# Two splits of hidden rows placed earlier in the order of the first down product

## The chip, the cores and the metric

The kernel runs on one core of a Trainium2 chip. The metric is the device time of one execution in microseconds, the median of several runs. A core has engines with a queue of instructions each, worked off in order: PE (TensorE, matrix products; its weight loads are shown as PEld), DVE (VectorE), ACT (ScalarE), POOL (GpSimd) and SP, which here issues DMAs.

## What is computed

An mLSTM cell over 4 batches, 8 heads, 768 positions and 40 features a head, and behind it a feed-forward block with exact GELU: 320 features up to 2048 and down again to 320, for all 3072 tokens.

```python
for t in range(S):
    m_new = np.maximum(f_gate[:, :, t] + m, i_gate[:, :, t])
    f_stab = np.exp(f_gate[:, :, t] + m - m_new)
    i_stab = np.exp(i_gate[:, :, t] - m_new)
    C = f_stab * C + i_stab * np.einsum('bhd,bhe->bhde', vt, kt)
    n = f_stab * n + i_stab * kt
    h_tilde = np.einsum('bhde,bhe->bhd', C, qt)
    y[:, :, t] = sigmoid(o_gate[:, :, t]) * h_tilde / np.maximum(np.abs(nq), 1.0)
x = y.transpose(0, 2, 1, 3).reshape(B * S, H * D)
h = x @ w_in
g = 0.5 * h * (1.0 + erf(h / sqrt(2)))
out = g @ w_out
```

## The kernel before, in words

The 768 positions are worked in 6 chunks of 128. In each chunk the four batches make 512 tokens. While the feed-forward block of one chunk runs on PE, the cell of a later chunk is worked beside it. The order in which every engine gets its work is written out by hand: strings of words (FRONT for everything up to the end of chunk 0's feed-forward, then SECOND, LATER, LAST) are read by `play` (line 1019), and each word calls one step. An engine's queue is the order in which the steps issue instructions for it. Waits are set where data or a buffer asks for them.

The steps around the change, all in the last lines of FRONT, by their letters:

- F: the next row of the first down product (line 880). There are 16 rows, of 128 hidden features each, from 0 to 15; the order below counts them. A row adds to the four banks `po`, one for each batch. Rows 0 to 9 take g and w_out as they are (4 products, two passes each). Rows 10 to 15 are taken in three parts (12 products): hi of g by hi of w_out, rest of g by hi of w_out, low of g by lo of w_out (lines 885 to 889).
- z n: split of g for row n (`split_g`, line 863): hi on ACT (line 873), rest on DVE (line 874), low on ACT (line 875). The parts go to tiles `g_part`, four parts in each, which lie where the g of earlier rows was: those of z10 where rows 0 to 3 were, later ones where rows 4 to 7 and 8 to 11 were.
- a n,k and b n,k: hi and lo of k rows of w_out from row n on (`out_hi`, line 931, on ACT for rows from 8 on; `out_lo`, line 938, on DVE).
- K and J: conversion of the next row of w_out from raw 64-bit words. K (`conv_one`, line 397) is two operations on ACT, `sig` (404) and `pow` (405), J (`conv_two`, line 410) two on DVE (416, 419). There are two buffers each for sig and pow, so the sig of one row waits until line 419 of the row two before it has read its buffer. The last J of FRONT are those of rows 12 to 15, the last K those of rows 14 and 15.
- X n, Y n, R n, G n: of chunk 1's cell, batch n: turn_y (transposes on PE into `px`, line 708, and x_hi on ACT, 718; two px banks), finish (DVE, lines 685 to 690, and 699), split_x (DVE, 727 and 728, which read px), gate (ACT, 506).
- p, + and [ and B: DMAs issued by SP; p exchanges halves of gate values, + copies k and q of later chunks, [ loads blocks, B loads the decay weights W, on which POOL then applies masks (line 474).

```python
        hi, rest, low = first_parts_of[n] = parts_of
        whole = first_g.row(n)
        nc.scalar.activation(out=hi, in_=whole, func=AF.Copy, scale=PART)
        nc.vector.tensor_tensor(out=rest, in0=whole, in1=hi, op=OP.subtract)
        nc.scalar.copy(out=low, in_=whole)
```

Of the kernel before, what the change touches and what calls it, by code (L numbers as in the profile page):

```python
# [27 lines left out]
    g1 c1 J y1 s2 K x0 t3 x1 v2 g2 O4 J B4 g3 c2 y2 s3 B5 K x2 K L5 J T0 K v3 A y3 M1 x3 c3 G0 M0 H O7 O6 O5 J  # L28
    J i5 u0 L6 u1 K W0 J W1 I4 A K S0 T1 C0 J i6 V0 i7 u2 G2 K U M2 L7 S1 J G1 K U i8 W2 J i9 C1 T2 K
    M3 f2 S2 V1 Y0 T3 J Y1 C2 e W3 K K K J S3 J C3 f3 K X0 J K R0 J K J V2 K Y2 J J K  # L30
    K V3 X1 J K r F J K (0 )0 F J K F K J F X2 G3 F J K F Y3 R1 J K F p + + + + J F J a10,2 b10,2 z10 a12 b12 F X3 z11 F a13,3 b13,3 z12 F z13 [1 F B8 z14 F B9 R2 z15 F R3 B10 B11 F a8 b8 a9 b9 F"""
CELL = "MWGVYXRKQDCSht"

HI_AT = {3: ("w_out3", 0), 8: ("w_out3", 2), 4: ("w_out0", 0), 5: ("w_out0", 1), 6: ("w_out2", 0), 7: ("w_out2", 1), 9: ("f0", 0)}
# [1073 lines left out]
```

## Time and profile before

| what | value |
|---|---|
| median of 3 runs | 438.06 us (437.81 to 439.68) |
| the profiled execution | 439.45 us |
| its span, first to last instruction | 437.7 us |
| PE, PEld busy | 429.5 us (98%), 376.6 us (86%) |
| DVE, ACT, POOL busy | 295.6, 277.3, 50.0 us |
| first down product on PE | 86.7 to 120.1 us |
| rows 10 to 15 of it | 108.75 to 120.1 us |
| mean granted clock of TensorE | 0.999 of full speed |

All times of the profile are microseconds from the start of the span of one profiled execution. A line of the order of time has the start, the duration, the engine, the line of the kernel, the operation, the tile written and the tiles read, the shape and the count; in brackets how long the engine was idle before it and what is taken to have released it. Neighbouring like instructions are merged into one line, and consecutive instructions of one engine overlap a little, so the step from one start to the next can be shorter than the duration. Who released a wait is inferred; "issue" means that nothing the profile shows was waited for.

### The profile page before, as it was taken

What the parts mean: (1) busy time and instruction counts of PE and PEld (TensorE: products, weight loads), DVE (VectorE), ACT (ScalarE), POOL (GpSimd) and SP (SyncE); (2) the same over time, 40 slices, a digit from 0 to 9 for tenths busy, and PEclk for the clock granted to TensorE, in tenths of its full rate; (3) what the DMA queues carried; (4) which work ended last, traced back from release to release, by engine and by line L of the source; (5) the groups of instructions that cost most, each with busy time, mean ns of one, the idle gap of its engine ahead of it and who ended that gap; (6) DMA issues with size and microseconds to landing.
All of it is one profiled execution on the core that took longest, in us unless ns stands there. A gap on an engine that the chain in (4) does not pass through costs nothing.

```text
span 437.7 us, 13034 instructions
## 1 busy us (share of the span) xinstructions
PE 429.5 (98%) x5344; PEld 376.6 (86%) x5344; DVE 295.6 (68%) x680; ACT 277.3 (63%) x595; POOL 50.0 (11%) x77
## 2 busy tenths in 40 slices
PE   9999999999999999999999999999999999999996
PEld 8778778877888898988898988898988889979986
DVE  7897777797888697737587737596746586533330
ACT  3989999965898985128776228795247715243441
POOL 3000212000530041030041030040010000000000
PEclk9999999999999999999999999999999999999999
DMA  7998996477791493563483564481561400010001
GB/s 153 198 211 228 196 247 164 124 197 197 210 184 56 88 191 63 108 172 63 65 179 69 107 165 69 94 157 32 108 157 18 61 1 1 18 45 1 1 1 60
DMA packets 162267, 48.81 MB, mean 112 GB/s; under 512 B 147776, under 2 KB 155232, under 8 KB 162208
## 3 DMA queue, kind: packets, MB, share of 16 engines
q1 hardware_dynamic: 161888, 47.65, 50.3%
q8 instruction: 42, 0.69, 0.7%
q10 hardware_dynamic: 320, 0.33, 0.2%
q14 instruction: 17, 0.14, 0.1%
HBM read 43.84 MB, written 9.37 MB: 122 GB/s over the span
## 4 chain that ended last, share of the span: by engine, by line
PE 73%; DVE 2%; ACT 2%; DMA 1%; issue 1%; ACTq 0%
PE po L991 31%; PE pu L966 24%; PE pu L977 7%; PE ps L568 3%; PE pf L621 2%; PE ph L674 1%; PE po L888 1%; PE po L674 1%; PE px L708 1%; DMA bits<-in_moe_w_out_dram 1%; PE pf L632 1%; ACT w_out_part L935 0%; DVE pow L416 0%; DVE w_out L419 0%; ACT sig L404 0%
## 5 line engine op out<-in xcount | busy, mean ns | idle before, releaser
L991 PE MATMUL po<-w_out_part,g_parts 128*128 128x320 f32 x960 | 140.7, 303 | 0.0
L991 PEld LDWEIGHTS po<-w_out_part,g_parts 128*128 128x128 f32 x960 | 131.6, 189 | 5.9 <-issue 4.6
L986 DVE TENSOR_TENSOR g_parts<-g_whole,g_parts 128x512 fp32r<-128x512 f32 x80 | 56.2, 702 | 57.8 <-ACT g_parts L985 55.7
L984 ACT ACTIVATE g_whole<-pu 128x512 f32<-128x512 f32 x80 | 47.2, 590 | 73.1 <-PE pu L977 62.6
L985 ACT ACTIVATE g_parts<-g_whole 128x512 fp32r<-128x512 f32 x80 | 50.5, 631 | 8.3 <-PE po L991 5.1
L474 POOL TENSOR_SCALAR_AFFINE_SELECT W<-W 128x1024 f32<-128x1024 f32 (+2 forms) x20 | 22.8, 1146 | 191.0 <-DMA W<-M_d 116.5
L500 ACT ACTIVATE W<-W,aT 128x128 f32<-128x128 f32 x128 | 38.7, 388 | 0.4 <-POOL W L474 0.2
L987 DVE CAST g_parts<-g_whole 128x512 fp32r<-128x512 f32 x80 | 36.3, 454 | 0.0
L699 ACT COPY far<-ob 128x128 f32<-128x128 f32 x16 | 4.6, 290 | 32.8 <-DVE ob L690 32.8
L966 PE MATMUL pu<-x_hi,w_in_hi 128*128 128x512 f32 x80 | 24.2, 384 | 0.0
L966 PE MATMUL pu<-x_hi,hi_first 128*128 128x512 f32 x80 | 23.9, 380 | 0.0
L966 PE MATMUL pu<-x_low,w_in 128*128 128x512 f32 x80 | 23.8, 379 | 0.0
L966 PE MATMUL pu<-x_rest,hi_first 128*128 128x512 f32 x80 | 23.8, 379 | 0.0
L966 PE MATMUL pu<-x_low,w_in_lo 128*128 128x512 f32 x80 | 23.8, 379 | 0.0
L966 PE MATMUL pu<-x_rest,w_in_hi 128*128 128x512 f32 x80 | 23.8, 379 | 0.0
L888 PE MATMUL po<-w_out,g 128*128 128x320 f32 x80 | 22.0, 432 | 0.0
L404 ACT ACTIVATE sig<-bits 128x320 f32<-128x320 f32 (+1 forms) x26 | 15.2, 585 | 10.6 <-issue 6.1
L574 DVE TENSOR_TENSOR W<-ps,W 128x256 f32<-128x256 f32 (+1 forms) x48 | 17.7, 413 | 4.2 <-PE ps L568 4.0
L888 PEld LDWEIGHTS po<-w_out,g 128*128 128x128 f32 x80 | 15.0, 190 | 5.9
L512 DVE STREAM_TRANSPOSE kT<-blocks 128x512 f32<-128x512 f32 x16 | 11.3, 709 | 12.0 <-DMA blocks<-kq_d 11.8
L639 DVE TENSOR_TENSOR far<-pf,gT 128x164 f32<-128x164 f32 x32 | 8.4, 319 | 14.7 <-PE pf L632 11.4
L1015 ACT ACTIVATE o_sb<-po 128x320 f32<-128x320 f32 x20 | 7.5, 442 | 16.7 <-PE po L991 16.7
(196 smaller groups left out, 788.3 us busy)
## 6 DMA issues: line engine op xcount, KB each, us to landing
W<-M_d SPq DMA_DIRECT2D x16, 512.0 KB, 6.6
bits<-in_moe_w_in_dram SPq DMA_DIRECT2D x20, 256.0 KB, 4.7
bits<-in_moe_w_out_dram SPq DMA_DIRECT2D x16, 320.0 KB, 4.8
blocks<-kq_d SPq DMA_DIRECT2D x32, 128.0 KB, 3.5
ob<-in_o_gate_dram SPq DMA_DIRECT2D x24, 160.0 KB, 4.3
out_dram<-o_sb SPq DMA_DIRECT2D x36, 80.0 KB, 2.0
wide<-M_d SPq DMA_DIRECT2D x4, 512.0 KB, 4.8
kq_d<-in_k_dram SPq DMA_DIRECT2D x6, 320.0 KB, 4.8
```

The costliest lines, as they stand in the source:

```text
L404: nc.scalar.activation(out=s, in_=hi.bitcast(F32), func=AF.Copy, scale=2.0 ** -112)
L474: nc.gpsimd.affine_select(out=x, in_=x, compare_op=OP.is_ge, fill=1.0e30, base=base, pattern=[[0, H], [1, x.shape[2]]], channel_multiplier=-1)
L500: nc.scalar.activation(out=W[n][:, h, :], in_=src, func=AF.Exp, scale=-1.0, bias=aT[:, self.c, r:r + 1])
L574: nc.vector.tensor_tensor(out=w[r, :, t], in0=ps[i][hip][r, :, t], in1=w[r, :, t], op=OP.mult)
L888: nc.tensor.matmul(to, xs[k][:, b * L:(b + 1) * L], w, start=(n == 0 and k == 0), stop=(n == NF - 1 and k + 1 == len(xs)), skip_group_chec ...
L966: nc.tensor.matmul(in_pairs(pus[i][e]), w3(at[k])[n][:, e, i * P:(i + 1) * P], in_turns(x3[n][:, k, :]), start=(n == 0 and k == 0), stop=F ...
L977: nc.tensor.matmul(in_pairs(pus[i][e]), w3(r)[n][h, p % 2, i * P:(i + 1) * P], in_turns(x3[n][h, NX, :]), start=False, stop=(n == 2), skip ...
L984: nc.scalar.activation(out=whole, in_=self.pus[n // 4][n % 4 // 2][n % 2], func=AF.Gelu)
L985: nc.scalar.activation(out=hi, in_=whole, func=AF.Copy, scale=PART)
L986: nc.vector.tensor_tensor(out=rest, in0=whole, in1=hi, op=OP.subtract)
L987: nc.vector.tensor_copy(out=low, in_=whole)
L991: nc.tensor.matmul(in_pairs(self.po[t]), x[:, t * L:(t + 1) * L], in_turns(w), start=(n == 0 and k == 0), stop=(n == NF - 1 and k == 2), s ...
```

## The change

In the last line of FRONT, two words change place. z10 moves from behind `a10,2 b10,2` to directly behind the fifth F (row 4). z12 moves from behind `a13,3 b13,3` to in front of them, behind the tenth F (row 9), and the F of row 10 stands behind a13 and b13 as before.

```diff
-    K V3 X1 J K r F J K (0 )0 F J K F K J F X2 G3 F J K F Y3 R1 J K F p + + + + J F J a10,2 b10,2 z10 a12 b12 F X3 z11 F a13,3 b13,3 z12 F z13 [1 F B8 z14 F B9 R2 z15 F R3 B10 B11 F a8 b8 a9 b9 F"""
+    K V3 X1 J K r F J K (0 )0 F J K F K J F X2 G3 F z10 J K F Y3 R1 J K F p + + + + J F J a10,2 b10,2 a12 b12 F X3 z11 F z12 a13,3 b13,3 F z13 [1 F B8 z14 F B9 R2 z15 F R3 B10 B11 F a8 b8 a9 b9 F"""
```

On the engines this means: on ACT the hi and low of z10 stand directly behind the gate of batch 3 (line 506) and in front of the sig of row 14; the hi and low of z12 stand in front of the hi of w_out rows 13 to 15. On DVE the rest of z10 stands in front of the conversion of row 12, and the rest of z12 in front of the lo of w_out rows 13 to 15. The orders on PE, POOL and SP stay as they are.

## The prediction, made before the changed kernel was run

> **What bounds the kernel now.** I read the busy table first, then the waits and the order of time between 94 and 126 us, where the moved steps lie, engine by engine.
>
> ```profile
> PE 429.5 (98%) x5344; PEld 376.6 (86%) x5344; DVE 295.6 (68%) x680; ACT 277.3 (63%) x595; POOL 50.0 (11%) x77
> ```
>
> PE is busy 98% of the span, and the chain that ended last is PE from 113.88 us on almost without a break. So the change is worth what it does to PE's gaps in the first down product, and what it makes late behind that. The weight loads of that stretch (start, duration, operation, count, idle before):
>
> ```profile
> 106.16 0.41 PEld L708 LDWEIGHTS px<-ident,ob 128*128 128x128 f32 x2
> 106.64 1.92 PEld L888 LDWEIGHTS po<-w_out,g 128*128 128x128 f32 x8
> 108.75 0.62 PEld L888 LDWEIGHTS po<-w_out_part,g_part 128*128 128x128 f32 x4 [0.19 <-ACT g_part L873]
> 109.96 3.29 PEld L888 LDWEIGHTS po<-w_out_part,g_part 128*128 128x128 f32 x24 [0.59 <-DVE g_part L874]
> 113.87 6.00 PEld L888 LDWEIGHTS po<-w_out_part,g_part 128*128 128x128 f32 x44 [0.63 <-DVE g_part L874]
> ```
>
> 106.64 is row 9; 108.75 the first four products (hi) of row 10; 109.96 the other 8 of row 10, row 11 and the hi of row 12; 113.87 the rest of row 12 up to row 15, ending at 119.87. Three gaps: 0.19 (hi of z10 on ACT), 0.59 (rest of z10 on DVE), 0.63 (rest of z12 on DVE, which stands behind b13): 1.41 us. These are what the two moved steps could remove.
>
> Where z10 goes, on DVE and on ACT:
>
> ```profile
> 98.89 0.50 DVE L419 SCALAR_TENSOR_TENSOR w_out<-sig,pow 128x320 uint32<-128x320 uint32 x1
> 101.12 0.49 DVE L416 SCALAR_TENSOR_TENSOR pow<-sig,pow 128x320 uint32<-128x320 uint32 x1 [1.74 <-ACT pow L405]
> 101.64 0.50 DVE L419 SCALAR_TENSOR_TENSOR w_out<-sig,pow 128x320 uint32<-128x320 uint32 x1
> 102.71 0.49 DVE L685 SCALAR_TENSOR_TENSOR ob<-ob,far 128x320 f32<-128x320 f32 x1 [0.57 <-ACT ob L506]
> 104.96 0.55 DVE L728 CAST x_low<-px 128x384 fp32r<-128x384 f32 x1
> 105.43 0.48 DVE L416 SCALAR_TENSOR_TENSOR pow<-sig,pow 128x320 uint32<-128x320 uint32 x1
> 105.94 0.50 DVE L419 SCALAR_TENSOR_TENSOR w_out<-sig,pow 128x320 uint32<-128x320 uint32 x1
> 108.48 0.83 DVE L943 TENSOR_TENSOR w_out_part<-w_out,w_out_part 128x640 fp32r<-128x640 f32 x1
> ```
> ```profile
> 102.22 0.46 ACT L506 ACTIVATE ob<-ob 128x320 f32<-128x320 f32 x1
> 102.57 0.49 ACT L404 ACTIVATE sig<-bits 128x320 f32<-128x320 f32 x1
> 106.53 0.50 ACT L404 ACTIVATE sig<-bits 128x320 f32<-128x320 f32 x1 [2.98 <-issue]
> 107.41 0.76 ACT L935 CAST w_out_part<-w_out 128x640 fp32r<-128x640 f32 x1
> 108.07 0.63 ACT L873 ACTIVATE g_part<-g 128x512 fp32r<-128x512 f32 x1
> ```
>
> From L685 at 102.71 to L419 at 105.94 DVE runs without a gap. ACT's sig at 106.53 (row 15) has a buffer that row 13's L419 read last; that ends at 105.94 + 0.50 = 106.44, so the 2.98 us put down to "issue" are a wait for DVE. Behind it in ACT's queue stands a10 (107.41), which row 10 needs as well as z10. So the stretch is a loop: DVE's queue sets row 15's conversion, that sets a10, and a10 sets row 10.
>
> **The change, part by part.** No instruction is added or removed, and no DMA moves. SP's, POOL's and PE's orders are the same; moved are three instructions of z10 and three of z12.
>
> z10, ACT: hi and low go ahead of row 14's sig, to where L506 leaves ACT at 102.57: hi 102.57 to 103.20, low 103.10 to 103.71 (steps of 0.53 and 0.51 between starts, as at 108.07). Their buffer needs rows 0 to 3, whose products ended at 95.3: no wait.
>
> z10, DVE: the rest now stands in front of row 12's L416 (101.12) and waits for the hi, 103.20 + 0.03 (as at 110.51 to 110.54) = 103.24. Behind it in DVE's queue are row 12's two operations, finish 3 (L685 to L699), split_x 1 (L727, L728), and rows 13 to 15. L416 goes from 101.12 to 103.84 (0.60 a step, from 109.22 to 109.82), L419 to 104.36, L685 to 104.78 (0.42 later, as from 95.83 to 96.25). L685 ran at 102.71, so the 0.57 it waited is absorbed and +2.07 remains. Nothing up to L419 of row 13 has a gap to take it up: L728 ends at 107.58, row 13's L419 at 108.51.
>
> What is late next: turn_y 3 (the px at 106.16) takes the bank that L728 reads, so it starts at 107.63 and not 106.16: PE loses 1.47. Row 9 then runs 108.11 to 110.03. Row 15's sig on ACT: 106.53 + 2.07 = 108.60, a10 109.48 to 110.24. Row 10 starts 0.05 behind it (the latency from 108.70 to 108.75): 110.29, a gap of 0.26. z10 is long done, but a10 is not.
>
> From there the steps run as before without z10: b10 on DVE 110.55 to 111.38; row 10's low needs it: 110.29 + 8 x 0.137 (3.29 us for 24 loads) = 111.39, so 0.04 lost. ACT: a12 110.14, X3 110.53, z11 hi 110.91, low 111.44. z11's rest on DVE 111.70 to 112.39, needed at 112.53.
>
> z12: on ACT hi 111.95, low 112.47, then a13 at 112.98 (before 110.91) to 114.10. On DVE its rest runs 112.62 to 113.31, ahead of b13, and row 12 needs it only at 114.2: the 0.63 is gone. The price: b13 starts at 114.13 (before 112.06) and z13's rest behind it (1.10 a step) at 115.24 to 115.93. Row 13 starts at 115.27 and needs that rest at 115.82: 0.16 lost. z14 (DVE from 115.84) and z15 (117.38 to 118.06) come before 117.1 and 118.7, when their rows start.
>
> Sum of PE's gaps: 1.47 + 0.26 + 0.04 + 0.16 = 1.93 instead of 1.41: **+0.52 us** at the end of the first down product.
>
> Behind it DVE ends that stretch some 1.2 us later (z15's rest 117.38 instead of 116.22). What hides that:
>
> ```profile
> 128.35 1.11 DVE L639 TENSOR_TENSOR far<-pf,gT 128x164 f32<-128x164 f32 x4 [1.24 <-PE pf L632]
> ```
>
> DVE waits 1.24 us here for PE, which comes 0.52 later itself: 1.2 - 0.52 is less than 1.24, cost nothing. Without that cover it would be 0.7. The masks on POOL follow DMAs that the moved work doesn't touch.
>
> Bounds. Lower: if DVE were held for nothing, all three gaps go, -1.41. Upper: the gaps return nothing and the whole +2.07 reaches the end. I take +0.52, since each of its four terms is set by a wait that the rows show.
>
> The one price the rows don't settle: b13, z13 and z14 now run beside POOL's masks (114.67, 4.08 us for three, 1.36 each). z14 and z15 ran there before, at 114.67 and 116.22, in 0.69 and 0.68 us; z10 and z11, away from the masks, took 0.69: nothing. The two L943 of 128x320 from 117.75 took 0.67 each instead of 0.49 at 109.82: 0.18 each. For three operations 0 to 0.5 us; I take 0, as the same operation beside the same masks shows. The Trainium skill (SBUF — State Buffer, Who interferes with whom) says that a DVE operation with two SBUF inputs and a GpSimd operation that reads SBUF shut each other out for a whole instruction. By that rule the sum would be +3.2 (below); the 0.69 beside the mask speaks against it here.
>
> The profiled execution took 439.45 us with a span of 437.70. The sum makes that 438.2 and 440.0. The median of the runs is 438.06, 1.39 below the profiled one; on it the forecast is 438.06 + 0.52 = **438.6 us**.
>
> **Rivals.**
> Free room: ACT sits idle 2.98 us, DVE 1.74 and 0.57, so z10 would fit in for nothing and the three gaps go: 438.06 - 1.41 = 436.65. For it: the idle times are real. Against: DVE's lie in front of a wait for ACT, and the hi can't come before 103.20.
>
> Passed on: DVE's +2.07 reaches the end, since later gaps move rather than go (a13 is 2.07 later on ACT, and rows 13 to 15 hang on it): 440.1. For it: z13's rest has no slack. Against: row 12's gap of 0.63 ends with z12 ahead of b13.
>
> Masks in the way: b13 and z13 each wait out one mask of 1.36 us on POOL, so row 13 and all behind it come 2.72 later than forecast: 441.3, slower by 0.7%. It decides from 114.67 on, when the masks begin. For it: the slower L943 at 117.75. Against: z14's 0.69 beside the first mask. (It is what the rule of the Trainium skill, SBUF — State Buffer, named above, would do here.)
>
> No effect: a10 comes early enough for row 10, if row 15's sig isn't held by row 13's L419; the 1.47 before row 9 and the 1.41 saved cancel: 438.1.
>
> **How the numbers follow.** Forecast 0.60 (438.1 to 439.3 for half a microsecond on either side), free room 0.08, passed on 0.17, masks 0.07, no effect 0.08. Half a per cent, 2.2 us, is about what a measurement of this kernel can tell from no change (its three runs span 437.81 to 439.68). Free room and no effect stay within it; I leave 0.03 for faster. Passed on is at the edge: half its chance, with the masks, makes 0.16 slower. Within: 0.81. The range reaches from near free room to just past passed on, 437.0 to 440.5, and leaves out the masks and part of free room.
>
> **What would show it.** z10's L873 near 102.6 and L874 near 103.2; row 12's L416 near 103.8; the px of turn_y 3 on PE after a gap of some 1.5 us, near 107.6; a10 (L935, 128x640) near 109.5 and row 10 directly behind its end; no gap ahead of row 12's rest; the first pu load near 120.3 instead of 119.82. Wrong if L685 stays near 102.7, if PE shows no gap ahead of turn_y 3, if L943 or L874 take over 1 us (128x512) beside the masks, or if PE shows new gaps behind 120 us.

## The result

The changed kernel took 439.82 us (median of 22 runs, 438.12 to 442.16), the kernel before 438.31 us (22 runs, 437.24 to 440.1). The ratio is 1.0027 with a 95% interval from 1.0016 to 1.0039: slower by 0.7 to 1.7 us. The forecast was 438.6 us, on a median of 438.06, that is 0.52 us slower or a ratio of 1.0012. The direction was right and the time lies in the range. The size is two to three times what was forecast (1.2 us by the ratio, 1.5 by the medians), and the time lies outside the half microsecond on either side of the forecast, 438.1 to 439.3, to which the prediction gave its chance of 0.60.

The span of the profiled execution is 438.9 us instead of 437.7. Row 0 of the first down product begins at 87.04 us, 0.33 later than before (86.71). That is ahead of the first moved step, so times are best read from row 0 on. The weight loads in order of time (start, duration, operation, count, idle before):

```profile
108.02 0.20 PEld L708 LDWEIGHTS px<-ident,ob 128*128 128x128 f32 x2 [1.62 <-issue]
...
110.61 8.53 PEld L888 LDWEIGHTS po<-w_out_part,g_part 128*128 128x128 f32 x61 [0.39 <-ACT w_out_part L935]
119.31 1.52 PEld L888 LDWEIGHTS po<-w_out_part,g_part 128*128 128x128 f32 x11 [0.17 <-DVE g_part L874]
120.78 0.33 PEld L966 LDWEIGHTS pu<-x_hi,hi_first 128*128 128x128 f32 x2
```

The gaps of 0.59 and 0.63 that the change was about are gone. In their place stand 1.62 ahead of turn_y 3, 0.39 ahead of row 10, now waiting for a10 (L935) and not for z10, and 0.17 within row 15, whose rest is late. The 61 loads behind row 10's gap hide 0.14 more, at row 13's rest: they take 8.53 us, where 0.1375 each (5.50 us for 40 in a profile below) makes 8.39. From row 0 to the first load of chunk 1's up product (here 120.78) it takes 33.74 us instead of 33.11.

DVE and ACT in order of time show the loop at work:

```profile
103.57 0.69 DVE L874 TENSOR_TENSOR g_part<-g,g_part 128x512 fp32r<-128x512 f32 x1 [3.12 <-ACT g_part L873]
...
105.11 0.48 DVE L685 SCALAR_TENSOR_TENSOR ob<-ob,far 128x320 f32<-128x320 f32 x1
...
107.36 0.55 DVE L728 CAST x_low<-px 128x384 fp32r<-128x384 f32 x1
...
108.34 0.50 DVE L419 SCALAR_TENSOR_TENSOR w_out<-sig,pow 128x320 uint32<-128x320 uint32 x1
```
```profile
108.92 0.50 ACT L404 ACTIVATE sig<-bits 128x320 f32<-128x320 f32 x1 [2.67 <-issue]
...
109.80 1.15 ACT L935 CAST w_out_part<-w_out 128x640 fp32r<-128x640 f32 x2
```

DVE stands idle for 3.12 us with z10's rest at the head of its queue, though row 12's words were ready on ACT by 100.44 (its L405 ran at 99.86 for 0.58). Row 13's L419 ends at 108.84, and row 15's sig starts 0.08 later: the wait called "issue" is that buffer. L728 ends at 107.91, and turn_y 3 starts 0.11 behind it.

What the forecast had at nothing is on POOL, and on DVE beside it:

```profile
116.10 1.09 POOL L474 TENSOR_SCALAR_AFFINE_SELECT W<-W 128x1024 f32<-128x1024 f32 x1 [48.99 <-ACT g_part L873]
```
```profile
116.13 1.60 DVE L874 TENSOR_TENSOR g_part<-g,g_part 128x512 fp32r<-128x512 f32 x1
```

z14's rest starts 0.03 us after a mask and takes 1.60 instead of 0.69 us. z15's rest comes late behind it, which is row 15's gap.

### The profile page after: what moved, and what is told of

Same layout as the page of the kernel before. It is cut to its first block, busy times and chain, and to the rows that moved or that the text cites. A ratio compares the mean times of both kernels' runs of the same rounds, so it can differ in the third digit from the quotient of the medians.

```text
span 438.9 us, 13035 instructions
## 1 busy us (share of the span) xinstructions
PE 429.6 (98%) x5344; PEld 375.8 (86%) x5344; DVE 297.4 (68%) x680; ACT 277.5 (63%) x595; POOL 50.9 (12%) x77
## 4 chain that ended last, share of the span: by engine, by line
PE 74%; DVE 1%; ACT 0%; issue 0%; DVEq 0%
PE po L991 31%; PE pu L966 24%; PE pu L977 7%; PE po L888 3%; PE ps L568 3%; PE pf L621 2%; PE ph L674 1%; PE px L708 1%; PE po L674 1%; PE pf L632 1%; DVE g_part L874 0%; ACT g_part L873 0%; DVE ob L690 0%; DVE w_out L419 0%; DVE x_low L728 0%
## 5 line engine op out<-in xcount | busy, mean ns | idle before, releaser
L987 DVE CAST g_parts<-g_whole 128x512 fp32r<-128x512 f32 x80 | 37.6, 470 | 0.0
L699 ACT COPY far<-ob 128x128 f32<-128x128 f32 x16 | 4.6, 290 | 32.7 <-DVE ob L690 32.7
L639 DVE TENSOR_TENSOR far<-pf,gT 128x164 f32<-128x164 f32 x32 | 8.4, 318 | 14.7 <-PE pf L632 10.6
```

Source lines behind the costliest of these rows:

```text
L987: nc.vector.tensor_copy(out=low, in_=whole)
```

## The experiments

Two theories were tested against the trace of the changed kernel. The queue theory: z10's rest on DVE holds row 12's conversion, and through row 15's sig all that follows. The mask theory: in addition the later rests fall beside POOL's masks and are held by them. All ratios are to the kernel before, run beside each on the same chip.

**Only z10's rest put back.** Its hi and low stay early on ACT.

```diff
-        nc.vector.tensor_tensor(out=rest, in0=whole, in1=hi, op=OP.subtract)
+        if n != 10:
+            split_rest(n)
...
-a10,2 b10,2 a12 b12
+a10,2 b10,2 l10 a12 b12
```
(l10 calls split_rest(10); the order is otherwise that of the changed kernel. The edit moves line numbers behind it by some five.)

> The changed kernel with only the rest of z10 on DVE put back behind b10; hi and low of z10 stay early on ACT, z12 stays in front of b13. Queue theory (row 12's conversion held behind z10's rest on DVE is what costs): L685 back near 102.7, no gap of PE ahead of the px of turn_y 3, a10 near 107.4; row 10 starts directly behind row 9 and waits some 0.8 us for its rest (109.2 to 109.9 on DVE); row 12's gap gone. Gaps of PE some 0.7 instead of 1.41: about 0.6 us faster than before, ratio 0.9985. Rival (the two ACT operations ahead of row 14's sig are what costs): the gap ahead of turn_y 3 stays, ratio like the changed kernel, 1.0027.

> Hi and low of z10 early, its rest behind b10, z12 in front of b13, a second time. Queue theory: no gap ahead of turn_y 3, 0.4 to 0.8 us at row 10's rest, ratio 0.997 to 0.9985, at most 0.4 us behind the kernel with z10 between rows 13 and 15. Rival (chance): ratio 1.000 or above.

Ratios 0.9973 (0.9951 to 0.9996) and 0.9970 (0.9957 to 0.9984). L685 ran at 102.36 and 100.72 us and no gap stands ahead of turn_y 3. In the first profile row 10 waits 0.38 us for its rest, where 0.8 had been expected, and in the second for nothing, where 0.4 to 0.8 had been expected: there row 13's sig started 13.18 us after row 0 instead of 14.07, so the words of w_out had landed earlier. The weight loads of the second:

```profile
105.25 0.41 PEld L708 LDWEIGHTS px<-ident,ob 128*128 128x128 f32 x2
...
107.73 9.97 PEld L893 LDWEIGHTS po<-w_out_part,g_part 128*128 128x128 f32 x72
117.64 0.32 PEld L971 LDWEIGHTS pu<-x_hi,hi_first 128*128 128x128 f32 x2
```

All 72 loads of rows 10 to 15 run without a gap. The place of this one DVE instruction is the difference between slower and faster than before; the two ACT operations ahead of row 14's sig leave no gap on PE. The rival falls.

**Each move alone.** First z10, then z12, moved without the other.

```diff
-X2 G3 F J K F Y3
+X2 G3 F z10 J K F Y3
...
-a10,2 b10,2 z10 a12 b12
+a10,2 b10,2 a12 b12
```

> Only z10 moved, z12 behind a13 and b13 as before. Queue theory: the gaps ahead of turn_y 3 and row 10 as in the changed kernel (1.5 and 0.3), and row 12 waits some 0.75 us for its rest, since a13 and b13 come 2 us later and z12's rest stands behind them: 1.1 us slower than before, ratio 1.0025, and more if the masks on POOL stretch the operations behind. Rival (z12's place is what costs): no slower than before, ratio 1.000 or below.

Ratio 1.0023 (1.0005 to 1.0041). Gaps of 1.38 ahead of turn_y 3, 0.41 ahead of row 10 and 0.69 ahead of row 12's rest; z14's rest again 1.49 us long, beside a mask that began 0.15 us before it.

```diff
-z11 F a13,3 b13,3 z12 F z13
+z11 F z12 a13,3 b13,3 F z13
```

> Only z12 moved, z10 behind b10 as before. Queue theory: row 10's two gaps (0.19, 0.59) stay, row 12's 0.63 goes, at most 0.1 appears at row 13: 0.6 us faster than before, ratio 0.9986. Rival (z12's place pushes b13 and z13 under the masks): a gap of 0.5 us or more at row 13 or 14 and z13 or z14 on DVE over 1 us instead of 0.69: ratio 1.000 or above.

Ratio 0.9984 (0.9967 to 1.0002), so the gain is likely but not clear of chance. In its profile not only row 12's gap is gone:

```profile
108.60 9.97 PEld L888 LDWEIGHTS po<-w_out_part,g_part 128*128 128x128 f32 x72
118.51 0.33 PEld L966 LDWEIGHTS pu<-x_hi,hi_first 128*128 128x128 f32 x2
```

Row 10's two gaps are missing too. Row 13's sig started 13.34 us after row 0 here and 14.28 us in the profile of before, and a10 19.79 instead of 20.70: the words of w_out landed earlier in this execution, and nothing else of z10's side was changed. The 0.78 us of row 10's gaps, which the prediction took from one execution, vary with these transfers. (A second profile of the kernel before, in the run with the probe below, has 0.43 there and 0.65 at row 12.) z13's and z14's rests took 0.70 us each, so the rival's sign is absent.

**z10 two conversions later**, behind J of row 13 and ahead of K of row 15, with z12 as in the changed kernel.

```diff
-G3 F z10 J K F Y3 R1 J K F p
+G3 F J K F Y3 R1 J z10 K F p
```

> z12 as in the changed kernel; z10 two conversions later, between the J of row 13 and the K of row 15, where ACT waits some 3 us and DVE has let row 15's sig go already. Queue theory: nothing that row 15's sig or turn_y 3 needs is behind z10, so all three gaps of PE go and at most 0.2 appears: 1.2 us faster than before, ratio 0.997. Rival (any z10 ahead of the last conversions delays a10 as much as it gains): ratio 1.000 or above, with a10 near 109.5.

> z10 between row 13's J and row 15's K, z12 in front of b13, a second time. Queue theory with the masks: from row 0 to chunk 1's first up product 31.8 to 32.3 us, z13 to z15 done before the first mask; ratio 0.997 to 0.998. Rival (the gain of the first run is chance): ratio 1.000 or above.

Ratios 0.9983 (0.9963 to 1.0003) and 0.9974 (0.9963 to 0.9986). No gap is listed at any row of either profile, though in the second the 72 loads of rows 10 to 15 take 10.17 us instead of 9.97; z13's and z14's rests (1.28 us for two) and z15's (0.68) are unstretched in both. In the second profile they were not all done before the first mask, as had been expected: that mask began at 114.50, and z15's rest at 115.66, just ahead of the second mask (115.80). This kernel and the one with z10's rest put back beat both the kernel before and the changed one (of the four intervals only the first here reaches 1); these runs don't tell the two apart.

**The masks taken out**, in the changed kernel and in the kernel before.

```diff
- U0 u0 j2 o0 o1 K1 Q1 L2 M0 M1 D0 D1
+ U0 u0 j2 o0 o1 K1 Q1 L2 D0 D1
```

> The changed kernel without POOL's masks of batches 0 and 1 of chunk 2 (the three operations of line 474 that begin at 116.10 in the changed kernel); their part of the computation is left out. Mask theory (z14's rest took 1.60 us instead of 0.69 because the first mask held it): z14's and z15's rests back to 0.69, no gap of PE ahead of row 15, the lo of the last w_out rows some 1 us earlier on DVE against PE: 0.3 to 0.5 us below the changed kernel, ratio 1.0015 to 1.002. Rival (the masks are no cause): z14's rest stays above 1 us, or the time stays at 1.0027.

> The kernel before without the same masks; their part of the computation is left out. Mask theory: there z14 and z15 took 0.69 and 0.68 us, so nothing is held but the two L943 after them (0.67 to 0.49): ratio 0.9995 to 1.000. Rival (taking masks away is worth something in itself, by ACT no longer waiting for POOL): the same drop as in the changed kernel, 0.3 us or more, ratio 0.999 or below.

Ratios 1.0028 (1.001 to 1.0046) and 0.9999 (0.9974 to 1.0024). The trace of the first does what the mask theory says, on DVE and on PE:

```profile
115.92 1.29 DVE L874 TENSOR_TENSOR g_part<-g,g_part 128x512 fp32r<-128x512 f32 x2
118.06 0.68 DVE L874 TENSOR_TENSOR g_part<-g,g_part 128x512 fp32r<-128x512 f32 x1
```
```profile
111.01 5.50 PEld L888 LDWEIGHTS po<-w_out_part,g_part 128*128 128x128 f32 x40 [0.41 <-ACT w_out_part L935]
116.66 4.37 PEld L888 LDWEIGHTS po<-w_out_part,g_part 128*128 128x128 f32 x32 [0.15 <-DVE g_part L874]
```

z13 to z15 have their plain length, and what is left behind row 10 is one gap of 0.15 at row 13's rest, where the prediction had 0.16. From row 0 to chunk 1's first load it takes 33.43 us there, less than in any profile of the changed kernel (33.74, and 35.62 and 34.93 below). But the time didn't fall, which was the rival's sign: 440.93 us, beside 440.20 for the changed kernel among the same runs. The edit had an effect of its own: with no mask ahead of it on POOL, the product vw of batch 0 (line 539) ran in the middle of finish 3 on DVE and held it (POOL, then DVE):

```profile
105.16 0.87 POOL L539 TENSOR_TENSOR vw<-vb,ewT 128x328 f32<-128x328 f32 x1 [17.44 <-DVE w_out L419]
```
```profile
105.36 0.70 DVE L686 TENSOR_SCALAR den<-far 128x8 f32<-128x8 f32 x1
```

L686 takes 0.17 us in the kernel before. From L685 to row 13's L416 it took 3.24 us there instead of 2.71 in the changed kernel, and 3.19 instead of 2.72 in the kernel before without masks (vw at 103.63; there the copy L699 took 0.70 instead of 0.23). That this is all that kept the time up is not shown. So the times of this pair don't settle what the masks cost; the forecast of 1.0015 to 1.002 for the first is neither shown nor refuted, and the second agrees with its forecast, but its interval is too wide to tell it from the rival's 0.999.

**The changed kernel again**, twice, unedited.

> The changed kernel once more, for a second profile and a time beside the other kernels of this call. Queue theory: from row 0 of the first down product to the first weight load of chunk 1's up product 33.5 to 33.9 us (33.74 in the first profile, 33.11 in the kernel before), z10's rest in front of row 12's conversion after an idle time of DVE of 2 us or more, ratio 1.002 to 1.004. Mask theory: z13's, z14's or z15's rest above 1 us if the first mask begins between their starts. Rival (the +0.63 of the first pair of profiles is chance): a stretch of 33.1 or less.

> The changed kernel a third time, beside the two kernels that place z10 better. Queue theory with the masks: the gap ahead of turn_y 3 of 1.4 to 2.3 us and one ahead of row 10; z13's, z14's or z15's rest above 1 us when a mask begins before it, with a gap of PE behind it; ratio 1.001 to 1.004, and the two others at least 0.3% below it. Rival (no difference beyond chance): all three within 0.2% of each other.

Ratios 1.0010 (0.9994 to 1.0026) and 1.0038 (1.0022 to 1.0053). The stretch from row 0 to chunk 1's first load was 35.62 and 34.93 us. So the second profile lies above the expected 33.5 to 33.9 us (the rival had 33.1 or less), while its ratio is below the expected 1.002 and not clear of 1; the third met its expectation. In both the first mask began ahead of z13's rest. DVE and POOL of the third profile, then its weight loads:

```profile
114.12 3.06 DVE L874 TENSOR_TENSOR g_part<-g,g_part 128x512 fp32r<-128x512 f32 x2
118.04 1.04 DVE L874 TENSOR_TENSOR g_part<-g,g_part 128x512 fp32r<-128x512 f32 x1
```
```profile
113.30 4.41 POOL L474 TENSOR_SCALAR_AFFINE_SELECT W<-W 128x1024 f32<-128x1024 f32 x3 [46.23 <-DMA W<-M_d]
```
```profile
106.58 0.20 PEld L708 LDWEIGHTS px<-ident,ob 128*128 128x128 f32 x2 [1.55 <-issue]
...
109.18 5.50 PEld L888 LDWEIGHTS po<-w_out_part,g_part 128*128 128x128 f32 x40 [0.41 <-ACT w_out_part L935]
115.74 2.88 PEld L888 LDWEIGHTS po<-w_out_part,g_part 128*128 128x128 f32 x21 [1.06 <-DVE g_part L874]
119.13 1.52 PEld L888 LDWEIGHTS po<-w_out_part,g_part 128*128 128x128 f32 x11 [0.51 <-DVE g_part L874]
```

z13 and z14 take 3.06 us for two where the kernel with z10 later takes 1.28, and PE waits 1.06 at row 13 and 0.51 at row 15. Rows 13 and 15 lose 1.57 us in this execution and 1.55 in the second; less the 0.15 that row 13 loses without masks, these are worth some 1.4 us in both, and 0.17 in the first. In the profile of before there was nothing of the kind, and in a second one (the run with the probe below) z15's rest took 0.90 us beside a mask without a gap on PE; the stretch from row 0 was 32.97 us there, so the 33.11 was no lucky execution. In the eleven profiles with masks the first one began 27.6 to 29.3 us after row 0, with no order between the kernels, and most of them name the DMA that loads W as what released it: what the change moved are the rests, not the masks.

**The lock by itself.** Behind the last step of the kernel before, DVE works operations with two SBUF inputs and then copies from PSUM, each alone and beside masks.

```diff
+    probe_one(1)
+    probe_two(6)
+    probe_masks()
+    probe_two(8)
+    probe_masks()
+    probe_one(8)
```
(probe_masks: a small memset on DVE that four masks on POOL wait for; probe_two: a subtraction of two SBUF operands; probe_one: a copy from PSUM.)

> The kernel before with a measurement behind its last step: on DVE a copy from PSUM, six subtractions of 128x328 with two SBUF inputs alone, then eight of them while POOL works four masks of 128x1024, then eight copies of 128x328 from PSUM while POOL works four masks again. Mask theory (a DVE operation with two SBUF inputs and a POOL operation that reads SBUF shut each other out for a whole operation): the subtractions take some 0.45 us alone, and beside the masks some of them 1 us or more, or the masks grow from 1.09 to 1.5 us; the copies from PSUM are as long as the one alone. Rival (no lock): the same durations in all parts.

One execution, in order of time, first DVE and then POOL:

```profile
435.73 3.17 DVE L1092 TENSOR_TENSOR vb<-blocks 128x328 f32<-128x328 f32 x6
...
438.93 7.31 DVE L1092 TENSOR_TENSOR vb<-blocks 128x328 f32<-128x328 f32 x8
...
446.27 4.23 DVE L1096 COPY vb<-probe_bank 128x328 f32<-128x328 f32 x8
```
```profile
439.07 5.21 POOL L1087 TENSOR_SCALAR_AFFINE_SELECT wide<-wide 128x1024 f32<-128x1024 f32 x4 [115.64 <-DVE wide L1085]
446.33 4.57 POOL L1087 TENSOR_SCALAR_AFFINE_SELECT wide<-wide 128x1024 f32<-128x1024 f32 x4 [2.04 <-DVE wide L1085]
```

Six subtractions alone take 3.17 us, 0.53 each from start to start. Beside four masks eight take 7.31, and those that meet a mask 1.27 each: DVE and POOL go in turns, one operation of each every 1.30 us. The eight copies from PSUM take 4.23 us, 0.53 each, beside masks that take 1.09. So the subtractions with two SBUF inputs are held, by 0.77 us for each mask, and the copies from PSUM are not. The rival falls. (The Trainium skill, SBUF — State Buffer, Who interferes with whom, states that a DVE operation with two SBUF inputs contends with a GpSimd operation that reads SBUF; the runs agree.) The probe has no operation with a single SBUF input. In the kernel, L727, which reads one operand from PSUM and one from SBUF, kept its length beside a mask (0.54 us at 117.66 in the changed kernel, 0.55 at 104.50 before, away from masks), but L686 and L699, which read one operand, from SBUF, were held by vw in the runs without masks. So two SBUF inputs are not the only case that is held.

## Why the prediction was right in kind and short in size

- **z10's rest holds DVE; L685 late by 2.07.** Right. From row 0, L685 came at 16.00 us before (102.71 - 86.71) and 18.07 in the changed kernel (105.11 - 87.04): 2.07. Undoing this one instruction's place turned 1.0027 into 0.997.
- **turn_y 3 loses 1.47, row 10 another 0.26 to a10.** Right: idle 1.62 and 0.39, and 1.55 and 0.41 in the third profile. These are idle times of the weight loads; 0.21 of the first and 0.08 of the second were already there as the plain steps around turn_y and from row to row, which leaves 1.41 and 0.31 in the first profile. The 0.04 at row 10's low didn't show. The second profile has 2.27 ahead of turn_y 3, with row 13's sig 14.94 us after row 0 instead of 14.26: there the words landed late.
- **Row 12's 0.63 goes, 0.16 comes at row 13.** Right: no gap at row 12 in any profile with z12 in front of b13, and at row 13 0.14 in the first profile and 0.15 with the masks out.
- **The masks cost nothing.** Wrong, and this is the term of the sum that was mis-sized. The prediction said of b13, z13 and z14 beside POOL's masks: "For three operations 0 to 0.5 us; I take 0, as the same operation beside the same masks shows." The row it rested on is z14's 0.69 in the profile of before, which began at 114.67 together with the first mask. Taken one by one, POOL and DVE of that profile show what the merged rows hid:

```profile
114.67 1.65 POOL L474 TENSOR_SCALAR_AFFINE_SELECT W<-W 128x1024 f32<-128x1024 f32 x1 [46.56 <-ACT g_part L873]
```
```profile
114.67 0.69 DVE L874 TENSOR_TENSOR g_part<-g,g_part 128x512 fp32r<-128x512 f32 x1 [0.25 <-ACT g_part L873]
...
117.75 0.48 DVE L943 TENSOR_TENSOR w_out_part<-w_out,w_out_part 128x320 fp32r<-128x320 f32 x1
118.15 0.95 DVE L943 TENSOR_TENSOR w_out_part<-w_out,w_out_part 128x320 fp32r<-128x320 f32 x1
```

The first mask took 1.65 us and not 1.09: here POOL was the one that waited. (The prediction's 1.36 is a mean over masks of three forms, 1.65, 1.57 and 0.84.) And of the two L943, which the prediction put at 0.67 each, the first ran its plain 0.48 and the second, begun behind the mask of 117.91, took 0.95. It was the same in the probe: the subtraction ahead of the first mask kept its 0.50, and that mask took 1.30. In the changed kernel the rests come 1 to 2 us later, against masks that come when they did, and meet masks already running: some 0.17, 1.4 and 1.4 us of PE's time in three profiles. That this is what the measured times have beyond the 0.52 is argued from these profiles; the pair without masks did not show it in the times. The rival of the masks had the mechanism, but named b13 and z13, where z13's, z14's and z15's rests were held and b13 took 1.16 us as ever, and its price of 2.72 us was too high; it was given 0.07.
- **The cover at L639.** Right without the masks (DVE still waited 0.99 us for PE there), and 0.45 us of it was left in the second and third profiles of the changed kernel, where PE itself was later. In the first profile of the changed kernel DVE came to L639 (129.68) without a wait, its last lo of w_out ending at 129.76, 2.65 us later than before instead of 1.2. From chunk 1's first up product (119.82, then 120.78) to the last chunk's down product (420.64, then 421.90) it took 0.30 us more; how much of that is this lateness was not tried.
- **The rivals and the range.** The time is nearer to the 440.1 of "passed on" than to the forecast, but not by that rival's mechanism: a13 did come 2.09 us later on ACT from row 0 (26.29 instead of 24.20), as the forecast had it too, yet row 12's gap went, and row 13 lost more than 0.15 only where a mask held its rest. The range held the time partly by luck: it left the masks out, and they happened to cost less than the 2.72 us of their rival.
- **The sum.** 0.52 forecast, 0.63 between the first two profiles from row 0 on, 1.8 and 2.5 to the other two, and 0.7 to 1.7 in the times. The gaps of the changed kernel hang on when the words of w_out and the decay weights land, and those of before do too; one pair of profiles gives the mechanism well and the mean badly.

## What to carry to other kernels

Moving an instruction earlier in an in-order queue moves its wait there as well: look at what the queue worked in that time, not whether the engine was idle. Here the early operation was free on the engine that had its input and expensive on the one that waited for it, and moving the two halves apart, or both behind the last step that the loop needs, gave what the change was after. When a sum pushes work into another engine's stretch, an operation that ran there unharmed may have been first; look whether the other one grew, and look at the operations one by one, since a merged row or a mean can hide the one that was held.

## What the runs showed of the hardware

A DVE operation with two SBUF inputs and a POOL mask took turns: 1.27 us for an operation that takes 0.50 alone and 1.23 to 1.30 for a mask that takes 1.09, while copies from PSUM kept 0.50. A start 0.03 us behind a mask of 1.09 us lost 0.91 (z14, 1.60 us), and a start together with one lost nothing (0.69, the mask 1.65). Two operations of DVE with one SBUF operand were held too, by a POOL product of two SBUF operands: L686 (0.70 instead of 0.17) and L699 (0.70 instead of 0.23).
